# Spectral mixing and a leaky-ReLU MLP: zero-tile matmuls and a reordered prologue

## The chip, the cores and the metric

The kernel runs on one core of one Trainium2 chip. The metric is the device time of one execution in microseconds (us), lower is better. Engines are named as in the profile: PE is TensorE, ACT is ScalarE, DVE is VectorE, POOL is GpSimd and SP is SyncE. Each runs its own list of instructions in the order in which the program wrote them; waits between them are semaphores.

## The reference

The input x has 8 batches of 3008 positions with 256 features. Every feature column is transformed along the positions, multiplied by a complex filter, and transformed back. The result is 24,064 tokens of 256 features for a two-layer MLP.

```python
X = np.fft.rfft(x, axis=1)
F = (filt_r + 1j * filt_i)[None, :, :]
y = np.fft.irfft(X * F, n=x.shape[1], axis=1)
h = y.reshape(B * S, D) @ w_in            # 256 -> 2048
out = np.maximum(0.01 * h, h) @ w_out     # 2048 -> 256
```

Inputs and output are float32; inside, the kernel works in float16 with float32 accumulation.

## The kernel before, in words

**Two kinds of work.** The transform is split as 3008 = 94 x 32 and done by matmuls against constant matrices. The MLP works on 47 chunks of 512 tokens. While the MLP of one batch runs, the transform of the next is threaded into it by a table of slots (`plan`, lines 399 to 412, run by the loop at line 424). Only the first batch has nothing to hide behind: its transform is written out by hand, lines 314 to 345, and is called the prologue here. The change touches only the prologue and the loads ahead of it.

**The stages of the prologue.** The 256 features are cut in two halves of 128 (`hf` 0 and 1), so that one half can be loaded while the other is worked on.

- **S1** (`first_s1`, line 247, matmuls at line 251): 94-point transforms. Eight groups per half, four 128-column matmuls each, from x_sb and the constant f1_sb into a PSUM bank. ACT or DVE then copies the bank into big[0] (`spread`, line 181). Groups 0 to 3 need the first half of x's columns, groups 4 to 7 the second.
- **T1** (`t1_part`, line 193): DVE transposes of 32x32 blocks, two per half, after all eight copies.
- **S2** (`first_s2`, line 256, matmuls at line 260): 32-point transforms of 4 or 8 columns of frequencies, then both products with the filters. On the POOL path ACT copies the bank to an SBUF tile fx of the pool's tags p1 and p2 (line 268, two buffers each) and POOL multiplies (line 271). On the DVE path DVE multiplies from PSUM (line 276). S2(hf, c) is written for the call that begins with column c: c = 8 and 20 of half 0 and c = 8 of half 1 go to POOL, the others to DVE. All S2 results share the two wide banks, named ph. The products are called fy.
- **upper** (line 306): copies a filter half from partitions 0 to 63 to 64 to 127, fa on ACT and fb on DVE (line 308), once that half is loaded. The products need it.
- **SA** (`first_sa`, line 279, matmuls at line 284): the inverse 32-point transform of fy, two accumulating matmuls of 512 columns for four columns of frequencies, copied by ACT into big[2] (line 285).
- **T2** (`first_t2`, line 292): four transposes on DVE, parts 0 and 1 after all SA of half 0, parts 2 and 3 after half 1.
- **SB** (`first_sb`, line 294, matmuls at line 301): inverse 94-point transforms in 16 groups, copied into yt (line 304), groups 0 to 7 by ACT and 8 to 15 by ACT and DVE in turn. With the last copy the MLP's first matmuls (line 365) can run.
- **keep_warm** (line 311): matmuls whose result nobody reads, into po_ps; before, they read small_sb and i1_sb.

**The loads.** SP issues the four parts of f1_sb and small_sb. POOL issues all others, in this order: two x loads of half 0, two each of fa and fb of half 0 (`filt_load`, line 137), the same six for half 1, then i1_sb and w_in_sb. POOL's transfers have eight completion semaphores in turn, so the ninth transfer is issued after the first has landed, and so on. In the kernel before the ninth is the first fa load of half 1.

The order around the change in the kernel before is: S1, T1, upper and S2 of half 0; the eight S1 groups of half 1; x_load(1); T1 of half 1; upper(1); SA(0,0) and SA(0,16); S2(1,8) and S2(1,0); SA(0,8) and SA(0,20); S2(1,16); SA of half 1 with T2; SB.

Of the kernel before, what the change touches and what calls it, by code (L numbers as in the profile page):

```python
# [10 lines left out]
P = 128  # L11
FP16 = mybir.dt.float16
# [6 lines left out]
N1, N2 = 94, 32  # L19
NC = 24  # L20
Q = 32
R1 = 96
# [43 lines left out]
def kernel(  # L66
# [9 lines left out]
    nc = tc.nc  # L76
    B, N, D = x.shape
# [5 lines left out]
    CH = 512  # L83
# [11 lines left out]
    i1_sb = cpool.tile([P, N2, N1], FP16, name="i1_sb")  # L95
    small_sb = cpool.tile([P, 3, P], FP16, name="small_sb")
# [5 lines left out]
    big = [cpool.tile([P, Q * D], FP16, name=f"big{i}") for i in range(3)]  # L102
# [3 lines left out]
    scrp = ctx.enter_context(tc.tile_pool(name="scr", bufs=2))  # L106
# [7 lines left out]
    po_ps = psp.tile([P, 2, D], FP32, name="po_ps")  # L114
    turn = {"ph": 0, "pf": 0}

    def bank(kind, n, w):
        of = wide if kind == "ph" else single
        t = of[turn[kind] % len(of)]
        turn[kind] += 1  # L120
        return t[:, : n * w].rearrange("p (n w) -> p n w", n=n)
# [4 lines left out]

    DH = D // 2

    def x_load(b, n0=0, nn=N2, d0=0, dn=D):

        for lo, cnt in ((0, R1),) if b + 1 < B else ((0, 64), (64, N1 - 64)):
            nc.gpsimd.dma_start(  # L132
                x_sb[lo : lo + cnt, ds(n0, nn), ds(d0, dn)],
                bass.AP(tensor=x.tensor, offset=x.offset + (b * N + lo * N2 + n0) * D + d0,
                        ap=[[N2 * D, cnt], [D, nn], [1, dn]]))

    def filt_load(dst, src, d0, dn):

        for q, first, sgn in ((0, 0, 1), (Q, N1, -1)):
            nc.gpsimd.dma_start(  # L140
                dst[q : q + Q, :, ds(d0, dn)],
                bass.AP(tensor=src.tensor, offset=src.offset + first * D + d0,
                        ap=[[N1 * D, N2 // 2], [sgn * NC * D, 2], [sgn * D, NC], [1, dn]]))
# [5 lines left out]
    nc.sync.dma_start(small_sb[:], small_d.ap())  # L149
    for hf in range(2):  # L150
        for n0 in (0, N2 // 2):
            x_load(0, n0, N2 // 2, hf * DH, DH)
        filt_load(fa_sb, filt_r, hf * DH, DH)
        filt_load(fb_sb, filt_i, hf * DH, DH)
    nc.gpsimd.dma_start(i1_sb[:], i1_d.ap())
# [2 lines left out]
    one = cpool.tile([1, 1], FP32, name="one")  # L158
    nc.vector.memset(one[:], 0.0)
    nc.scalar.activation(one[:], one[:], AF.Lrelu)  # L160

    nc.vector.memset(big[2][:].rearrange("p (e n t) -> p e n t", n=Q, t=2)[:, :, NC:Q, :], 0.0)


    def s1_group(b, g, copy=nc.scalar.copy):
# [10 lines left out]
    def paired(t):  # L176
        return t[:].rearrange("p (e n t) -> p n e t", n=Q, t=2)

    def spread(dst, n0, ps, copy, e0=0):
        nn, de = ps.shape[1], ps.shape[2] // 2  # L180
        copy(paired(dst)[:, ds(n0, nn), ds(e0, de)], ps.rearrange("p n (e t) -> p n e t", t=2))  # L181
# [3 lines left out]
    def t1_part(b, i, flat=False):  # L185
        def go():
            a = big[(4 * b) % 3][:].bitcast(FP32)[:, ts(i, E4 * Q)].rearrange("p (e n) -> p e n", n=Q)
            o = big[(4 * b + 1) % 3][:].bitcast(FP32)
            if flat:
                o = o[:, ts(i, E4 * Q)].rearrange("p (e n) -> p e n", n=Q)  # L190
            else:
                o = o.rearrange("p (n e) -> p e n", n=Q)[:, ts(i, E4), :]
            nc.vector.transpose(o, a)  # L193
        return go
# [52 lines left out]
    def first_s1(hf, g, kind, copy):  # L247
        ps = bank(kind, 4, DH)
        for j in range(4):
            n2 = 4 * g + j  # L250
            nc.tensor.matmul(ps[:, j, :], f1_sb[:N1, n2, :], x_sb[:N1, n2, ts(hf, DH)],  # L251
                             start=True, stop=True)
        spread(big[0], 4 * g, ps, copy, hf * DH // 2)


    def first_s2(hf, c, n, on_pool):
        ps = bank("ph", n, DH)
        src = paired(big[1])
        for j in range(0, n, 4):
            nc.tensor.matmul(ps[:, ds(j, 4), :].rearrange("p n (e t) -> p n e t", t=2), fwd2,  # L260
                             src[:, ds(c + j, 4), ts(hf, DH // 2)], start=True, stop=True)
        fs = [f[:, ds(c, n), ts(hf, DH)] for f in (fa_sb, fb_sb)]
        if on_pool:
            y = [outp.tile([P, n, DH], FP16, tag="ost", name=f"fy{i}_h{hf}_c{c}") for i in range(2)]
            xs = [scrp.tile([P, 4, DH], FP32, tag=f"p{j // 4 + 1}", name=f"fx_h{hf}_c{c + j}")
                  for j in range(0, n, 4)]
            for j, xf in enumerate(xs):
                act(xf[:], ps[:, ts(j, 4), :])
            for i in range(2):
                for j, xf in enumerate(xs):  # L270
                    nc.gpsimd.tensor_tensor(y[i][:, ts(j, 4), :], xf[:], fs[i][:, ts(j, 4), :], AL.mult)
        else:
            y = [ypp.tile([P, n, DH], FP16, tag=f"yw{i}", bufs=2, name=f"fy{i}_h{hf}_c{c}")
                 for i in range(2)]
            for i in range(2):
                nc.vector.tensor_tensor(y[i][:], ps, fs[i], AL.mult)  # L276
        ys[(hf, c)] = y

    def first_sa(hf, c):
        y = ys.pop((hf, c))  # L280
        for j in range(0, y[0].shape[1], 4):
            ps = bank("pf", 4, DH)
            for i, m in enumerate((inv2, inv2x)):
                nc.tensor.matmul(ps, m, y[i][:, ds(j, 4), :], start=(i == 0), stop=(i == 1))  # L284
            act(paired(big[2])[:, ds(c + j, 4), ts(hf, DH // 2)],
                ps.rearrange("p n (t e) -> p n e t", t=2))
# [7 lines left out]
    def first_sb(g, copy, kind):  # L294
        dt, h = g // 8, g % 8
        src = big[0][:].rearrange("p (h n e r t) -> p h n r t e", h=2, n=Q // 2, r=2, t=2)
        ps = bank(kind, 4, N1)
        for j in range(4):
            n2 = 4 * h + j
            for t in range(2):  # L300
                nc.tensor.matmul(ps[64 * t : 64 * t + 64, j, :], src[:, dt, n2 // 2, n2 % 2, t, :],  # L301
                                 i1_sb[:, n2, :], start=True, stop=True)
        yv = yts[0][:, dt, :].rearrange("p (a c) -> p a c", c=N2)
        copy(yv[:, :, ds(4 * h, 4)], ps.rearrange("p c a -> p a c"))  # L304

    def upper(hf):
        for t, cp in ((fa_sb, act), (fb_sb, dve)):
            cp(t[64:P, :, ts(hf, DH)], t[0:64, :, ts(hf, DH)])


    def keep_warm(n):
        for _ in range(n):
            nc.tensor.matmul(po_ps.rearrange("p a d -> p (a d)"), small_sb[:, 0, :],  # L313
                             i1_sb[:].rearrange("p a d -> p (a d)")[:, 0:512],
                             start=True, stop=True)

    for g in range(8):
        first_s1(0, g, two[(g // 2) % 2], (act, dve)[g % 2])
    t1_part(0, 0, True)(), t1_part(0, 1, True)()
# [1 line left out]
    first_s2(0, 8, 8, True)  # L321
    first_s2(0, 0, 8, False)
    first_s2(0, 20, 4, True)
    first_s2(0, 16, 4, False)
    for g in range(8):
        first_s1(1, g, two[g % 4 == 3], dve if g in (3, 5, 7) else act)
    x_load(1)
    t1_part(0, 2, True)(), t1_part(0, 3, True)()
    upper(1)
    first_sa(0, 0), first_sa(0, 16)  # L330
    first_s2(1, 8, 8, True)
    first_s2(1, 0, 8, False)
    nc.gpsimd.dma_start(w_out_sb[:], moe_w_out.rearrange("(ct p) d -> p ct d", p=P))
    first_sa(0, 8), first_sa(0, 20)
    first_s2(1, 16, 8, False)
    first_sa(1, 0)
    first_t2(0), first_t2(1)
    first_sa(1, 16), first_sa(1, 8)
    first_t2(2), first_t2(3)
    keep_warm(5)  # L340
    for g in range(8):
        first_sb(g, act, two[(g // 2) % 2])
    keep_warm(3)
    for g in range(8, 16):
        first_sb(g, (act, dve)[g % 2], two[(g // 2) % 2])

# [52 lines left out]
    def plan(b, s1, per, t1, s2, step, lag, t2, sb):  # L399
        for g in range(16):  # L400
            at(s1 + g // per, s1_group(b, g, dve if b == 1 and g % 2 else act))
        if b + 1 < B:
            at(s1 + 15 // per, lambda: x_load(b + 1))
        for i in range(4):
            at(t1 + i, t1_part(b, i))
        for g in range(12):
            at(s2 + (step * g) // 4, s2_group(b, g))
            at(s2 + lag + (step * g) // 4, sa_group(b, g))
        for i in range(4):
            at(t2 + i, t2_part(b, i))  # L410
        for g in range(16):
            at(sb + g // 2, sb_group(b, g, dve))
# [6 lines left out]
    for slot in range(SL * (NCHUNK + 1)):  # L419
        ci, g = divmod(slot, SL)  # L420
# [36 lines left out]
```

## Time and profile before

| what | value |
|---|---|
| median of 3 runs | 785.25 us (784.58 to 785.80) |
| profiled execution, own time | 787.67 us |
| its span | 785.9 us |
| PE busy | 763.0 us, 97% of the span |
| ACT, DVE, POOL busy | 557.0, 365.1, 150.7 us |
| first S1 matmul | 9.59 us |
| first S2 matmul | 17.67 us |
| first SB matmul | 39.80 us |
| end of the last yt copy of the prologue | 45.98 us |

Times in the trace are counted from the start of the span. A row of the timeline gives the start, the duration, the engine and line, and what was written from what. "x8" at its end means that eight like instructions were merged, and the brackets give the idle time of that engine just before and what ended it. The names of tiles are shown without their numbers, so big, pf, ph and yt stand for several buffers.

### The profile page before, as it was taken

The page shows a single profiled execution, that of the slowest core. Times are in us where ns is not written, and L with a number is a line of the kernel's source. Part 1 is how long each engine was busy: PE and PEld are TensorE (multiplying, and loading weights), DVE is VectorE, ACT ScalarE, POOL GpSimd, SP SyncE. Part 2 cuts the span into 40 slices and gives each one's busy share as a digit, 9 for nine tenths or more (in the row PEclk, how much of TensorE's full clock was granted, in tenths as well). Part 3 has the DMA queues.
Part 4 walks back from the last instruction along what each step waited for, and adds up shares of the span by engine and source line. Part 5 has one row for each costly group of instructions (what it writes and reads, how often), then busy time and mean ns, then how long its engine had stood idle before and what let it go on. Part 6 is the DMA issues. An engine that isn't in the chain of part 4 may idle for free.

```text
span 785.9 us, 13623 instructions
## 1 busy us (share of the span) xinstructions
PE 763.0 (97%) x5812; PEld 528.6 (67%) x5812; DVE 365.1 (46%) x459; ACT 557.0 (71%) x794; POOL 150.7 (19%) x122
## 2 busy tenths in 40 slices
PE   2799999999999999999999999999999999999998
PEld 1356677666776677866777667776677667676666
DVE  3869760784327652387316754078432765200000
ACT  3686768676687767877687775967668776666664
POOL 5773400240003400052001410024000340000000
PEclk9999999999999999999999999999999999999999
DMA  9943010501032010501014101050100101101111
GB/s 174 214 59 94 28 42 28 122 28 41 28 79 70 28 41 28 119 31 41 28 41 108 41 28 41 28 120 28 42 28 28 41 28 42 41 28 41 41 41 54
DMA packets 42013, 43.39 MB, mean 55 GB/s; under 512 B 14274, under 2 KB 40514, under 8 KB 41282
## 3 DMA queue, kind: packets, MB, share of 16 engines
q0 software_dynamic: 15760, 16.99, 13.2%
q1 hardware_dynamic: 26192, 25.53, 9.3%
q8 instruction: 45, 0.74, 0.4%
q14 instruction: 16, 0.13, 0.1%
HBM read 34.10 MB, written 24.64 MB: 75 GB/s over the span
## 4 chain that ended last, share of the span: by engine, by line
PE 93%; ACT 2%; issue 1%; DVE 0%; ACTq 0%; DVEq 0%
PE po_ps L379 41%; PE ph L365 40%; PE pf L170 3%; PE pf L237 2%; PE pf L210 2%; PE pf L225 2%; PE pf L379 1%; ACT big L181 1%; ACT gt_c L370 1%; PE pf L284 1%; PE ph L260 0%; PE ph L301 0%; DVE fy_h_c L276 0%; PE po_ps L313 0%; PE pf L301 0%
## 5 line engine op out<-in xcount | busy, mean ns | idle before, releaser
L370 ACT ACTIVATE gt_c<-ph 128x1024 f16<-128x1024 f32 x376 | 384.8, 1024 | 194.8 <-PE ph L365 193.8
L365 PE MATMUL ph<-yt,w_in_sb 128*128 128x512 f16 (+7 forms) x1728 | 386.6, 351 | 0.4 <-ACT yt L304 0.2
L379 PE MATMUL po_ps<-w_out_sb,gt_c 128*128 128x256 f16 x2944 | 381.5, 272 | 0.6 <-ACT ost_c_t L386 0.6
L379 PEld LDWEIGHTS <-gt_c 128*128 128x128 f16 x3008 | 290.7, 98 | 86.7 <-issue 1.7
L365 PEld LDWEIGHTS <-w_in_sb 128*128 128x128 f16 x1728 | 163.0, 98 | 95.2 <-issue 1.0
L218 POOL TENSOR_TENSOR y_b_g<-p_b_g,p_b_g 128x512 f16<-128x512 f32 x84 | 106.9, 1273 | 225.5 <-DVE p_b_g L216 225.5
L181 ACT CAST big<-pf 128x512 f16<-128x512 f32 x195 | 111.8, 606 | 11.8 <-PE pf L251 11.7
L193 DVE STREAM_TRANSPOSE big<-big 128x1024 f32<-128x1024 f32 x32 | 55.8, 1846 | 127.1 <-ACT big L181 126.7
L240 DVE CAST yt<-pf 128x376 f16<-128x376 f32 x112 | 56.3, 545 | 85.9 <-PE pf L237 85.9
L214 DVE TENSOR_TENSOR p_b_g<-pf,fa_sb 128x512 f32<-128x512 f32 x84 | 58.1, 692 | 38.0 <-PE pf L210 35.5
L386 ACT COPY ost_c_t<-po_ps 128x256 f32<-128x256 f32 x184 | 69.4, 377 | 6.7 <-PE po_ps L379 5.6
L201 DVE STREAM_TRANSPOSE big<-big 128x1024 f32<-128x1024 f32 x28 | 51.1, 1936 | 34.5 <-ACT big L181 34.5
L215 DVE TENSOR_TENSOR p_b_g<-pf,fb_sb 64x512 f32<-64x512 f32 x84 | 58.2, 693 | 1.1
L216 DVE TENSOR_TENSOR p_b_g<-pf,fb_sb 64x512 f32<-64x512 f32 x84 | 57.4, 683 | 1.1
L132 POOL DMA_DIRECT2D x_sb<-in_x_dram x12 | 8.5, 713 | 256.6 <-PE pf L170 255.5
L237 PEld LDWEIGHTS <-big 128*128 128x128 f16 x448 | 25.7, 98 | 13.2
L170 PE MATMUL pf<-x_sb,f_sb 94*128 94x256 f16 x224 | 33.8, 272 | 0.1
L210 PE MATMUL pf<-big,small_sb 128*128 128x512 f16 x84 | 31.8, 379 | 0.0
L225 PE MATMUL pf<-y_b_g,small_sb 128*128 128x512 f16 x84 | 31.8, 379 | 0.0
L237 PE MATMUL pf<-i_sb,big 128*128 128x94 f16 x448 | 28.7, 206 | 0.0
L170 PEld LDWEIGHTS <-f_sb 94*128 94x128 f16 x224 | 21.0, 97 | 9.5 <-issue 1.3
L347 POOL TENSOR_SCALAR fb_sb<-fb_sb 64x6144 f16<-64x6144 f16 x1 | 15.7, 15742 | 0.4 <-DVE fy_h_c L276 0.4
(45 smaller groups left out, 142.8 us busy)
## 6 DMA issues: line engine op xcount, KB each, us to landing
out_dram<-ost_c_t SPq DMA_DIRECT2D x92, 256.0 KB, 2.1
x_sb<-in_x_dram POOLq DMA_DIRECT2D x6, 1536.0 KB, 11.3
x_sb<-in_x_dram POOLq DMA_DIRECT2D x4, 384.0 KB, 11.0
w_in_sb<-in_moe_w_in_dram POOLq DMA_DIRECT2D x1, 1024.0 KB, 14.9
w_out_sb<-in_moe_w_out_dram POOLq DMA_DIRECT2D x1, 1024.0 KB, 10.2
x_sb<-in_x_dram POOLq DMA_DIRECT2D x1, 1024.0 KB, 9.1
f_sb<-fwd_const SPq DMA_DIRECT2D x4, 192.0 KB, 3.2
fa_sb<-in_filt_r_dram POOLq DMA_DIRECT2D x4, 192.0 KB, 9.8
```

The source lines that it names most:

```text
L170: nc.tensor.matmul(ps[:, j, :], f1_sb[:N1, n2, :], x_sb[:N1, n2, :], start=True, stop=True)
L181: copy(paired(dst)[:, ds(n0, nn), ds(e0, de)], ps.rearrange("p n (e t) -> p n e t", t=2))
L214: nc.vector.tensor_tensor(p1[:], ps, fa, AL.mult)
L215: nc.vector.tensor_tensor(p2[0:64], ps[64:P], fb[64:P], AL.mult)
L216: nc.vector.tensor_tensor(p2[64:P], ps[0:64], fb[0:64], AL.mult)
L218: nc.gpsimd.tensor_tensor(y1[:], p1[:], p2[:], AL.add)
L237: nc.tensor.matmul(ps[:, j, :], src[:, dt, n2, :], i1_sb[:, n2, :], start=True, stop=True)
L240: copy(yv[:, :, ds(4 * h, 4)], ps.rearrange("p c a -> p a c"))
L365: nc.tensor.matmul(ph[:, j, ds(o, ln)], w_in_sb[:, dt, ts(ct, P)], yts[b % 2][:, dt, ds(lo, ln)], start=(dt == 0), stop=(dt == NDT - 1),)
L370: nc.scalar.activation(gts[ci][:, ds(2 * g, 2), :], ph, AF.Lrelu)
L379: nc.tensor.matmul(po, gts[ci][:, ct, ts(tj, P)], w_out_sb[:, ct, :], start=(ct == 0), stop=(ct == NCT - 1))
L386: nc.scalar.copy(ost[:, tj % 2, :], po)
```

## The change

- 24 matmuls of a zeroed 128x512 tile are issued on PE ahead of everything else. The tile, `idle`, is a buffer of tag p1; one memset on DVE fills it, and the memset of big[2] follows after it. `keep_warm` now reads this tile, also in its later use.
- The two x loads of half 0 are each cut into two, of 64 and of 32 partitions. So there are four x loads ahead of the filters, and the ninth transfer on POOL is the first x load of half 1.
- upper(1) moves from after T1 of half 1 to before S1 of half 1.
- S2(0,16) moves from before S1 of half 1 to between its groups 2 and 3.
- S2(1,16) moves ahead of SA(0,8) and SA(0,20).
- keep_warm(3) between SB groups 7 and 8 is removed.

```diff
-    def x_load(b, n0=0, nn=N2, d0=0, dn=D):
+    def x_load(b, n0=0, nn=N2, d0=0, dn=D, parts=None):
 
-        for lo, cnt in ((0, R1),) if b + 1 < B else ((0, 64), (64, N1 - 64)):
+        if b + 1 < B:
+            parts = parts or ((0, R1),)
+        for lo, cnt in parts or ((0, 64), (64, N1 - 64)):
...
         for n0 in (0, N2 // 2):
-            x_load(0, n0, N2 // 2, hf * DH, DH)
+            x_load(0, n0, N2 // 2, hf * DH, DH, None if hf else ((0, 64), (64, 32)))
...
-    nc.vector.memset(big[2][:].rearrange("p (e n t) -> p e n t", n=Q, t=2)[:, :, NC:Q, :], 0.0)
...
     def keep_warm(n):
         for _ in range(n):
-            nc.tensor.matmul(po_ps.rearrange("p a d -> p (a d)"), small_sb[:, 0, :],
-                             i1_sb[:].rearrange("p a d -> p (a d)")[:, 0:512],
+            nc.tensor.matmul(po_ps[:].rearrange("p a d -> p (a d)"), idle[:, 0:P], idle[:],
                              start=True, stop=True)
 
+    idle = scrp.tile([P, CH], FP16, tag="p1", name="idle")
+    nc.vector.memset(idle[:], 0.0)
+    keep_warm(24)
+
+    nc.vector.memset(big[2][:].rearrange("p (e n t) -> p e n t", n=Q, t=2)[:, :, NC:Q, :], 0.0)
...
     first_s2(0, 20, 4, True)
-    first_s2(0, 16, 4, False)
+    upper(1)
     for g in range(8):
+        if g == 3:
+            first_s2(0, 16, 4, False)
         first_s1(1, g, two[g % 4 == 3], dve if g in (3, 5, 7) else act)
     x_load(1)
     t1_part(0, 2, True)(), t1_part(0, 3, True)()
-    upper(1)
     first_sa(0, 0), first_sa(0, 16)
     first_s2(1, 8, 8, True)
     first_s2(1, 0, 8, False)
     nc.gpsimd.dma_start(w_out_sb[:], moe_w_out.rearrange("(ct p) d -> p ct d", p=P))
+    first_s2(1, 16, 8, False)
     first_sa(0, 8), first_sa(0, 20)
-    first_s2(1, 16, 8, False)
...
         first_sb(g, act, two[(g // 2) % 2])
-    keep_warm(3)
```

## The prediction

> **What bounds the kernel now.** I read the page first, then the order of events in the first 60 us. The page says that TensorE (PE) is busy 97% of the span, and its strip of 40 slices has only two slices short of full, the first 39 us. From the chain of waits, PE carries everything from 56.7 us to the end without a gap, so nothing touched by this change can alter that stretch; the change can only move the moment at which it begins. The prediction is therefore about the prologue, which ends with the last copy into yt at 45.98.
>
> From the page:
>
> ```profile
> PE   2799999999999999999999999999999999999998
> ```
>
> The timeline of VectorE (DVE), prologue rows (start, duration, what, idle before):
>
> ```profile
> 17.55 0.95 DVE L308 COPY fb_sb<-fb_sb 64x3072 f16<-64x3072 f16 x1
> 20.78 1.22 DVE L276 TENSOR_TENSOR fy_h_c<-ph,fb_sb 128x1024 f16<-128x1024 f32 x1
> 22.68 0.69 DVE L276 TENSOR_TENSOR fy_h_c<-ph,fa_sb 128x512 f16<-128x512 f32 x1 [0.68 <-PE ph L260]
> 26.88 2.37 DVE L193 STREAM_TRANSPOSE big<-big 128x1024 f32<-128x1024 f32 x2
> 29.29 0.96 DVE L308 COPY fb_sb<-fb_sb 64x3072 f16<-64x3072 f16 x1
> 31.29 1.23 DVE L276 TENSOR_TENSOR fy_h_c<-ph,fa_sb 128x1024 f16<-128x1024 f32 x1 [1.04 <-ACT fx_h_c L268]
> 34.70 1.22 DVE L276 TENSOR_TENSOR fy_h_c<-ph,fa_sb 128x1024 f16<-128x1024 f32 x1 [1.06 <-PE ph L260]
> ```
>
> PE, the same stretch:
>
> ```profile
> 12.45 1.01 PE L251 MATMUL pf<-x_sb,f_sb 94*128 94x128 f16 x8 [0.99 <-DMA x_sb<-in_x_dram]
> 22.05 0.59 PE L260 MATMUL ph<-big,small_sb 128*128 128x512 f16 x1 [1.61 <-DVE fy_h_c L276]
> 29.31 1.88 PE L260 MATMUL ph<-big,small_sb 128*128 128x512 f16 x4 [1.33 <-DVE big L193]
> 31.02 2.74 PE L284 MATMUL pf<-fy_h_c,small_sb 128*128 128x512 f16 x6
> 34.41 1.04 PE L284 MATMUL pf<-fy_h_c,small_sb 128*128 128x512 f16 x4
> ```
>
> The reader should see three things. The second-half S1 groups wait at 22.05 behind one S2 matmul that DVE releases. The last S2 (L260, 33.55) waits behind six SA matmuls, so DVE starts its last products only at 34.70. And PE runs at half speed: four 128x512 matmuls take 1.88 us (0.43 each) until about 34.2, then four take 1.04 (0.22 each beyond the last one's tail).
>
> The arrivals of the filters, not marked in those rows, decide my forecast. The DMA answer for the window around 14.1 us is
>
> ```profile
> fb_sb<-in_filt_i_dram POOLq DMA_DIRECT2D x2, 192.0 KB, 10.6
> ```
>
> The two are the second-half fb loads, issued at 13.39 and 14.10; with 10.3 and 10.8 us to landing they are there at 23.7 and **24.9**. The second-half fa loads (9.84 + 11.7 and 12.69 + 9.9) land at 21.5 and 22.6, the second-half x loads at 18.3 and 21.1. In the kernel before these are wanted at 26.3 (ACT) and 29.3 (DVE), so they hide.
>
> **The skill.** "TensorE: Matmul & The Clock Gate", Part 1 (the HAM clock gate): a matmul takes N/1.2 ns while cold and N/2.4 + 2.5 ns warm, warmth needs a busy window of about 3.4 us, and an idle window returns it to cold. The trace agrees on the prices (0.43 and 0.22 us at N = 512); how long warmth outlasts sparse work no row of before shows. The same page, under the array's architectural detail, says that ACT and DVE are strict FIFO; the rows agree, each engine's order being the program's. "DMA: Bandwidth & Descriptors", Anatomy of one DMA: the semaphore follows the last byte by most of a fixed 2 us. Here the queue carries a steady 717 packets per us from 8 to 22 us; the 256-byte packets (12,288) are through at about 22.7 and the last filter load lands at 24.9, 2.2 later.
>
> **The change, part by part.**
>
> *24 zero matmuls.* They start after one small memset, about 1.4 us. All cold: 24 x 0.427 = 10.2, ending at 11.6; warm after 3.4 to 6.8 us: 7 to 8.5. First x lands at 9.6. If warm, S1's second quarter finishes sooner (16 matmuls at about 0.06 instead of 0.107), so DVE's last copy starts about 13.8 instead of 14.36, the transpose at 14.5 instead of 15.15, four S2 matmuls take 0.87 instead of 1.71, and DVE's fy pair ends near 20.4 instead of 22.0. Gain here 1.6, all spent by the next part. If cold: gain 0, same end.
>
> *upper(1) moved ahead of the second-half S1.* The built order puts DVE's fb copy between fy(0,0) and fy(0,16), and ACT's fa copy ahead of all its second-half S1 copies. DVE stands from 20.4 until the fb load lands, 24.9. Queued behind it on DVE: fy(0,16), three S1 copies, the transpose. So 24.95 + 0.93 copy, + 2 x 0.60 products, + 3 x 0.60 S1 copies, last one's tail: transpose at **29.0** instead of 26.88. ACT waits to 22.6, copies until 25.4, and its five S1 copies (0.53 each, two held by buffers) end by 28.3, under DVE's 28.9. Loss: 2.1. The copy no longer stands at 29.29, but DVE was idle there.
>
> *S1 groups 0 to 2 ahead of S2(0,16).* They run at 19 to 20 instead of 22.46; worth nothing, since ACT copies them only after 25.4.
>
> *idle holds one of the two p1 buffers* until its last use. The order shows fx(0,20) now waiting on POOL: three products of 1.11 from about 18.2, so 21.6. ACT's next item waits to 22.6 anyway: 0.
>
> *S2(1,16) ahead of SA(0,8), SA(0,20).* Transpose ends 29.0 + 2.37 = 31.4. Four S2 matmuls, cold: 1.71 + 0.18, fy(1,0) at 33.35 (31.29 before). S2(1,16) follows when ACT has emptied its buffer, 33.6 to 34.5, so DVE goes straight on: fy(1,16) at 33.35 + 2.28 = **35.65**, against 34.70. The six SA matmuls (2.56) no longer stand in DVE's way. Recovered: 1.15 of the 2.1.
>
> *End of the prologue.* fy(1,16) ends 38.0; SA(1,16) and SA(1,8), eight warm matmuls, 38.1 to 39.8 (38.8 before); keep_warm(5) 1.08; SB at 41.0 (39.80 before). ACT's eight yt copies (0.37 each) pace what follows, so dropping keep_warm(3) gives back only 0.1 to 0.4 of its 0.75. Sum: +1.2 - 0.2 = +1.0.
>
> *First x load split.* Issue of 1,536 descriptors takes 1.08, of 768 0.71, so 64 rows about 0.83: the first piece leaves 0.25 earlier. But PE needs both pieces, and the queue is saturated later. The x second-half loads are now issued after the first piece lands (about 9) instead of at 6.3; packets ahead of them last to 14, so nothing starves. Bounds -1.3 (packets at the full rate from 4 us on) to +1 (a queue that starves once); I take 0, because the filters' last packet is set by the sum of the packets.
>
> *x_load(1), w_out, the fb negation on POOL:* each about 2 later at most; x lands about 41 for use at 47.7, w_out at 48 for 59, the negation ends 54 for use at 66. Hidden; the next wait they could cause is PE's S1 of batch 1, 5 us away.
>
> The profiled execution has 787.67 for a span of 785.9; it becomes about 788.7. The runs' median is 785.25, so **786.3**. About 0.2% (1.6 us) is what a measurement can tell here.
>
> **Rivals.**
> 1. *PE stays cold longer, clearly slower.* PE has almost nothing from 22.8 to 26 (S1 group 4 needs ACT's first copy), so warmth is lost; in before it took from 29.31 to 34.2 to come back, and the denser start is now 31.4 or 33.6. If it returns at 38 the loss is 1.6, at 40 2.4, at 42 3.4: SA(1,16), SA(1,8) and the five warmers then run at 0.43. It decides above 0.2% from 38 us on. For it: 33.6 plus 4.9 is 38.5. Against: SA runs from 28.3 already.
> 2. *Warm throughout: no change.* Zero matmuls and the earlier S1 keep the clock: S2(1,x) takes 0.87, fy(1,0) at 32.5; total +0.2, with the edge of an earlier issue 0.0 to 0.2: 785.3. Against: the idle stretches of 3.5 us near 13.5 to 17 and of 3 near 23.
> 3. *Transfers earlier: faster.* Two pieces in flight fill the queue from 4 us; all landings 1.3 earlier, the DVE wait ends at 23.6, and with it total 0.0 (cold) to -1.1 (warm): 784.2.
> 4. *The zero matmuls don't release the clock.* Then the first half is as before, fy ends 22.0, still before 24.9: the same +1.0, because DVE waits anyway.
>
> **How the numbers follow.** Forecast, with rival 4 in it (+0.3 to +1.5; own range 785.5 to 786.8): 0.50. Rival 1 (+1.6 to +3.4): 0.27. Rival 2: 0.13. Rival 3: 0.05. A loss that I don't see, over 1.6: 0.05. Slower by over 0.2%: 0.27 + 0.05 + 0.03 of the forecast's upper edge = 0.35. Faster: most of rival 3 and a little for a gain I don't see, 0.06. Within: 0.59. The range, 784.7 to 788.3, holds the forecast, rival 2 and rival 1 up to a loss of 3.0.
>
> **What would show it.** DVE's second fb copy starting at 24.5 to 25, with some 4 us of idle ahead put down to the fb load; the second transpose pair near 29.0; the last fy pair following the one before without a gap, at 35.7; SB's first matmul near 41. Wrong if the fb load lands before 23, if 128x512 matmuls take 0.22 from 31 us (rival 2) or still 0.43 after 38 (rival 1), or if PE's steady stretch after 57 us is itself longer.

## The result, and the profile after

The changed kernel takes **787.94 us** (median of 6 runs, 787.46 to 788.42). The kernel before, run beside it, takes 785.52 (6 runs, 784.58 to 787.19). The ratio is 1.0028, with a 95% interval of 1.0015 to 1.0041: slower by 2.2 us, between 1.2 and 3.2. The forecast was 786.3 in a range of 784.7 to 788.3. So the direction and the range held, and the likeliest case, +1.0, was too small by more than half. The prediction gave 0.59 to a change of at most 0.2% and 0.35 to a loss above that; 0.28% lies above it, though the interval reaches below.

The steady stretch is not the cause. From the end of the last yt copy to the end of the span there are 739.9 us in the kernel before (785.9 - 45.98) and 739.8 after (785.7 - 45.85). So the difference is to be looked for in the prologue. These two executions alone don't show it, since both prologues end near 45.9; the second profile of before, below, does.

The timeline of DVE after, the prologue rows that answer to those shown of before:

```profile
15.15 0.95 DVE L308 COPY fb_sb<-fb_sb 64x3072 f16<-64x3072 f16 x1
18.38 1.21 DVE L276 TENSOR_TENSOR fy_h_c<-ph,fb_sb 128x1024 f16<-128x1024 f32 x1
23.76 0.95 DVE L308 COPY fb_sb<-fb_sb 64x3072 f16<-64x3072 f16 x1 [4.16 <-DMA fb_sb<-in_filt_i_dram]
24.74 0.69 DVE L276 TENSOR_TENSOR fy_h_c<-ph,fa_sb 128x512 f16<-128x512 f32 x1
27.93 2.37 DVE L193 STREAM_TRANSPOSE big<-big 128x1024 f32<-128x1024 f32 x2
32.27 1.22 DVE L276 TENSOR_TENSOR fy_h_c<-ph,fa_sb 128x1024 f16<-128x1024 f32 x1 [1.97 <-PE ph L260]
34.54 1.21 DVE L276 TENSOR_TENSOR fy_h_c<-ph,fa_sb 128x1024 f16<-128x1024 f32 x1
```

DVE is done with the first products at 19.6 and then stands for 4.16 us until the second-half fb filter has landed. Everything behind the copy waits with it: the products of S2(0,16), three S1 copies, the transposes at 27.93. The last pair of products (34.54) follows the pair before without a gap.

ACT over the same stretch, after:

```profile
20.41 0.59 ACT L268 COPY fx_h_c<-ph 128x512 f32<-128x512 f32 x1 [3.02 <-POOL fy_h_c L271]
21.46 2.75 ACT L308 COPY fa_sb<-fa_sb 64x3072 f16<-64x3072 f16 x1 [0.47 <-DMA fa_sb<-in_filt_r_dram]
24.23 2.07 ACT L181 CAST big<-pf 128x512 f16<-128x512 f32 x4
```

ACT loses time in three places ahead of its first second-half S1 copy: 3.02 us for a buffer that POOL holds, 0.47 us for the fa load, and 2.75 us for the fa copy itself.

PE, after:

```profile
1.23 7.43 PE L313 MATMUL po_ps<-idle 128*128 128x512 f16 x24 [1.23 <-DVE idle L317]
10.63 0.61 PE L251 MATMUL pf<-x_sb,f_sb 94*128 94x128 f16 x8 [1.08 <-DMA x_sb<-in_x_dram]
15.26 1.88 PE L260 MATMUL ph<-big,small_sb 128*128 128x512 f16 x4 [3.58 <-DVE big L193]
24.89 1.57 PE L251 MATMUL pf<-x_sb,f_sb 94*128 94x128 f16 x12 [3.46 <-ACT big L181]
33.45 5.56 PE L284 MATMUL pf<-fy_h_c,small_sb 128*128 128x512 f16 x18
```

The zero matmuls do speed up S1 (0.61 us for eight instead of 1.01). S2 still takes 1.88 for four, as before. At 24.89 S1 group 4 of half 1 has stood for 3.46 us, until ACT could free a PSUM bank for it.

The chain of work that ended last says it in two rows (start, duration, what):

```profile
5.09 7.59 DMA fa_sb<-in_filt_r_dram
...
12.96 10.70 DMA fb_sb<-in_filt_i_dram
```

Two filter loads carry the chain from 5.1 to 23.7 us, with 0.28 us between them: a first-half fa load, whose landing lets POOL issue the second-half fb load, and then that load. The kernel before never waited for the second of them. It did not have it earlier either: in the second profile of before it was issued at 13.10 and took 10.6 us, so it landed at 23.7 too. What changed is not the load but the moment at which its copy is asked for.

### The profile page after: what moved, and what is told of

It is laid out like the page before. It is cut to its first block, busy times and chain, and to the rows that moved or that the text cites. A ratio compares the mean times of both kernels' runs of the same rounds, so it can differ in the third digit from the quotient of the medians.

```text
span 785.7 us, 13669 instructions
## 1 busy us (share of the span) xinstructions
PE 769.0 (98%) x5833; PEld 529.6 (67%) x5833; DVE 364.7 (46%) x460; ACT 556.9 (71%) x794; POOL 151.9 (19%) x124
## 4 chain that ended last, share of the span: by engine, by line
PE 93%; DMA 2%; ACT 2%; issue 1%; DVE 1%; POOL 0%; ACTq 0%; DVEq 0%; POOLq 0%
PE po_ps L383 41%; PE ph L369 40%; PE pf L170 3%; PE pf L237 2%; PE pf L225 2%; PE pf L210 2%; DMA fb_sb<-in_filt_i_dram 1%; DMA fa_sb<-in_filt_r_dram 1%; PE pf L383 1%; ACT big L181 1%; PE pf L284 1%; ACT gt_c L374 1%; POOL x_sb L134 0%; PE ph L260 0%; ACT yt L304 0%
```

## The experiments

Each ratio below is against the kernel before on the same chip, with its 95% interval; 0.1% is 0.79 us.

### The kernel before, once more

No edit. The profile of before that the prediction reads took 787.67, which is above all six runs of before in the result; this asks what another execution looks like.

> The kernel before once more, for a second profile. Theory F (filter wait: the change loses because upper(1) makes DVE wait for the second-half fb load) says nothing on it. Theory C (clock phase: the profile of before that the prediction read was one of the slow executions, and most executions of before get a warm PE earlier) expects a span of 783 to 784.5 instead of 785.9, the 128x512 matmuls of S2 in half 1 at 0.22 us instead of 0.43 or warming before 32 us, and the last yt copy ending at 43.5 to 45 instead of 45.98. If the profile is again at 45.9 to 46.1 and still cold to 34, C falls.

Measured: 785.76 against 786.07, ratio 1.0000 (0.9991 to 1.0010). The 35 runs of the kernel before on that chip lie between 784.06 and 788.12. This profile's own time is 784.98, its span 783.2. DVE of this execution of the kernel before:

```profile
25.33 2.37 DVE L193 STREAM_TRANSPOSE big<-big 128x1024 f32<-128x1024 f32 x2
...
30.86 1.21 DVE L276 TENSOR_TENSOR fy_h_c<-ph,fb_sb 128x1024 f16<-128x1024 f32 x1
32.00 1.22 DVE L276 TENSOR_TENSOR fy_h_c<-ph,fa_sb 128x1024 f16<-128x1024 f32 x1
```

and PE of the same execution:

```profile
29.45 1.48 PE L284 MATMUL pf<-fy_h_c,small_sb 128*128 128x512 f16 x6
30.77 1.02 PE L260 MATMUL ph<-big,small_sb 128*128 128x512 f16 x2
```

Same program, another prologue. The second transposes start at 25.33, not 26.88, because the first two x loads had landed at 8.55 and 10.89 instead of 9.59 and 12.45. And the six SA matmuls ahead of S2(1,16) take 1.48 us, not 2.74, so the gap of 1.06 us on DVE ahead of the last products (34.70 in the first profile) does not exist here: 32.00 follows directly. The windows of the two executions of before give the reason for the second difference. The columns are the stretch, its length, the busy times of PE, PE's weight loads, DVE, ACT and POOL, the granted clock (the share of TensorE's full clock that the profile records), the DMA share and GB/s. First the profile that the prediction used:

```profile
29.00:33.00 4.00, 3.69 (x9) 1.16 (x9) 2.93 (x4) 3.26 (x8) 1.79 (x2) 0.70 1.09 229
33.00:36.00 3.00, 2.48 (x9) 0.74 (x8) 1.94 (x3) 2.08 (x4) 3.00 (x4) 0.83 1.14 246
```

then this one:

```profile
29.00:33.00 4.00, 3.82 (x14) 1.23 (x12) 3.28 (x3) 3.15 (x7) 3.35 (x3) 1.00 1.12 237
```

The granted clock was 0.70 in one and 1.00 in the other. The last yt copy ends at 43.27 instead of 45.98. The kernel before has prologues that differ by 2.7 us, and the prediction was built on the long one. The second one is no norm either: its own time lies 0.8 below the median of its runs.

### The change with upper(1) back in its old place

Later texts call this kernel e2.

```diff
-    upper(1)
     for g in range(8):
...
     t1_part(0, 2, True)(), t1_part(0, 3, True)()
+    upper(1)
```

> The changed kernel with upper(1) back after T1 of half 1, all else as changed. Theory F: DVE's 4.2 us wait before the second fb copy goes, the second transpose pair starts at 23 to 25 instead of 27.93, the last yt copy ends 2 to 3.5 us earlier than in the changed kernel (42.5 to 44), time 784 to 785.7: 2.2 to 3.9 under the changed kernel's 787.9. Theory C (only clock phases differ): within 0.8 of the changed kernel.

Measured: 783.91 against 786.07, ratio 0.9982 (0.9974 to 0.9990), faster than before. DVE:

```profile
24.61 2.37 DVE L193 STREAM_TRANSPOSE big<-big 128x1024 f32<-128x1024 f32 x2
```

Everything else of the change together is worth -0.18%; with upper(1) early it is +0.28%. So the early upper costs 0.46%, 3.6 us, by these two ratios. In the profiles, the transposes move from 24.61 to 27.93 (3.3) and the last yt copy ends at 42.20 against 45.85 (3.6).

### upper(1) early, and nothing else

The kernel before, with upper(1) ahead of S2(0,16).

```diff
     first_s2(0, 20, 4, True)
+    upper(1)
     first_s2(0, 16, 4, False)
...
     t1_part(0, 2, True)(), t1_part(0, 3, True)()
-    upper(1)
```

> The kernel before with only upper(1) moved ahead of S1 of half 1. Theory F: DVE waits for fb (lands 24 to 25), the second transpose pair at 28.5 to 29.2 instead of 26.9, the six SA matmuls still ahead of S2(1,16); 1.0 to 2.5 slower than before: 786.5 to 788. Theory C: within 0.8 of before.

Measured: 789.56 against 786.07, ratio 1.0053 (1.0040 to 1.0067), +4.2 us by the ratio: more than expected. DVE:

```profile
25.03 1.41 DVE L308 COPY fb_sb<-fb_sb 64x3072 f16<-64x3072 f16 x1 [3.52 <-DMA fb_sb<-in_filt_i_dram]
...
29.66 2.37 DVE L193 STREAM_TRANSPOSE big<-big 128x1024 f32<-128x1024 f32 x2
```

The early copies, with nothing else of the change, give more than the whole loss. The load landed at 25.0 here and at 23.7 in the changed kernel, so the transposes are 4.3 later than in the second profile of before (25.33) and the last products, at 36.28 against 32.00, also 4.3.

### Which of the two copies does it

Two kernels, each the changed one with one of the two copies put back. `of` picks 0 for ACT's fa copy, 1 for DVE's fb copy.

```diff
-    def upper(hf):
-        for t, cp in ((fa_sb, act), (fb_sb, dve)):
+    def upper(hf, of=(0, 1)):
+        for t, cp in [((fa_sb, act), (fb_sb, dve))[i] for i in of]:
...
-    upper(1)
+    upper(1, (0,))          # fa early; the other kernel has (1,)
...
     t1_part(0, 2, True)(), t1_part(0, 3, True)()
+    upper(1, (1,))          # fb late; the other kernel has (0,)
```

Only ACT's fa copy early (e7):

> The changed kernel with only DVE's fb copy of upper(1) back after T1 of half 1; ACT's fa copy stays ahead of its S1 copies. Theory F-DVE (DVE's wait for fb carries the loss): DVE no longer stands, but ACT waits for fa to 21.5 and copies to 24.2, so S1's copies end near 27 and T1 starts at 26.5 to 27.2 instead of 27.9; 0.7 to 1.5 under the changed kernel: 786.4 to 787.2. Rival F-ACT (ACT's part carries it): within 0.4 of the changed kernel. Rival: ACT's part costs nothing: 784, as with upper(1) undone.

Measured: 787.49 against 785.68, ratio 1.0022 (1.0014 to 1.0030). DVE of that kernel:

```profile
26.23 0.69 DVE L181 CAST big<-pf 128x512 f16<-128x512 f32 x1 [3.85 <-PE pf L251]
...
27.88 2.37 DVE L193 STREAM_TRANSPOSE big<-big 128x1024 f32<-128x1024 f32 x2
```

and PE:

```profile
25.05 1.56 PE L251 MATMUL pf<-x_sb,f_sb 94*128 94x128 f16 x12 [3.47 <-ACT big L181]
```

Only DVE's fb copy early:

> The changed kernel with only ACT's fa copy of upper(1) back after T1 of half 1; DVE's fb copy stays early. With e7 this is the second half of the pair. Theory either (each early copy alone holds S1 as long as both): DVE waits for fb to 23.7, then fy(0,16), three S1 copies, T1 at 27.8 to 28.1; ACT's fa copy now stands between its S1 copies and the SA copies; 787.3 to 788.5. Theory F-ACT (only ACT's copy carries the loss): 784 to 785.

Measured: 788.47 against 785.33, ratio 1.0036 (1.0022 to 1.0050). DVE and then PE of that kernel:

```profile
24.05 0.95 DVE L308 COPY fb_sb<-fb_sb 64x3072 f16<-64x3072 f16 x1 [4.23 <-DMA fb_sb<-in_filt_i_dram]
...
28.23 2.37 DVE L193 STREAM_TRANSPOSE big<-big 128x1024 f32<-128x1024 f32 x2
```

```profile
26.38 0.58 PE L251 MATMUL ph<-x_sb,f_sb 94*128 94x128 f16 x4 [3.04 <-DVE fy_h_c L276]
```

Either copy alone gives the loss of both, within the intervals, with the transposes at 27.88 and 28.23 against 27.93. With fa early ACT frees its first S1 bank late, PE waits for the bank, and DVE waits 3.85 us for PE. With fb early DVE waits for the load and PE for DVE. The two waits stand side by side, so taking one away gains nothing that clears the intervals. A reader who sees only the 4.16 us on DVE, and moves only that copy back, gets nothing for it.

### The other parts, one at a time

The zero tile, its 24 matmuls and keep_warm reading it, on the kernel before (keep_warm's operands and the place of big[2]'s memset as in the change, not shown again):

```diff
+    idle = scrp.tile([P, CH], FP16, tag="p1", name="idle")
+    nc.vector.memset(idle[:], 0.0)
+    keep_warm(24)
```

> The kernel before with only the zero tile, its 24 matmuls and keep_warm reading it. The 24 take 7 to 10 us and end before the first S1; S1 at 0.06 us a matmul instead of 0.107; the first S2 at 17.0 instead of 17.67. Theory F: 0 to 0.7 faster than before, since the first half has little slack without the early upper. Theory C: the clock is the whole difference, so this alone changes the time by over 1 us either way. If the idle buffer matters (fx(0,20) waits for POOL), ACT's third fx copy starts near 22 instead of 20.5 and S1 group 3 of half 1 shifts with it, cost up to 1.

Measured: 785.18 against 786.07, ratio 0.9992 (0.9982 to 1.0001). The 24 matmuls take 8.01 us; S1 follows them without a gap at 9.08, though the first x load had landed by 8.55, when POOL issued the load that waits for it. So here they hold the first four S1 groups up by some 0.5 us, which costs nothing, since the next four wait for x until 10.58. Eight S1 matmuls take 0.61. The second transposes start at 24.43, 0.9 earlier than in the second profile of before, but the six SA matmuls take 2.43 in this execution and DVE's last products start at 31.95, after 0.77 us of waiting for S2: 0.05 earlier than in that profile. The gain at the transposes was given back behind the SA matmuls.

The split x load, on the kernel before (with x_load's `parts` as in the change):

```diff
-            x_load(0, n0, N2 // 2, hf * DH, DH)
+            x_load(0, n0, N2 // 2, hf * DH, DH, None if hf else ((0, 64), (64, 32)))
```

> The kernel before with only the two x loads of half 0 cut into 64 and 32 partitions. Theory N (the cut is neutral: the packets' sum sets every arrival, and the arrivals differ from run to run anyway): within 0.7 of before, the second-half fb load landing at 23.5 to 25. Theory S (the cut brings the first x earlier, as the profile after the change seems to show, 8.49 against 9.59): 1 to 1.5 faster. A loss of over 0.7 would speak for the semaphores: the x loads of half 1 issued later, at 7.8 instead of 6.3, would then be late for S1.

Measured: 785.07 against 785.68, ratio 0.9997 (0.9989 to 1.0005): nothing. x is there at 8.68 and 10.97, against 8.55 and 10.89 in the second profile of before.

S2(1,16) ahead of SA(0,8) and SA(0,20), on the kernel before:

```diff
+    first_s2(1, 16, 8, False)
     first_sa(0, 8), first_sa(0, 20)
-    first_s2(1, 16, 8, False)
```

> The kernel before with only S2(1,16) ahead of SA(0,8) and SA(0,20). The prediction's sum gave it 1.15 with a PE that is cold to 34 us. Theory C: in most executions of before the clock is back by 30 us (as in the second profile of before), so that DVE's last two pairs already follow one another, and the gain is 0 to 0.5. If it is 1.0 or more, the prediction's size stands.

Measured: 785.00 against 785.68, ratio 0.9994 (0.9986 to 1.0003): 0.5 us faster, and the interval includes no change. In its profile the last products start at 31.69 without a gap; in the second profile of before there is none either.

The three, -0.08, -0.03 and -0.06%, add up to -0.17%. The kernel with upper(1) put back, which also lacks keep_warm(3) and has the other S1 order, has -0.18%. No run tests these two parts alone.

### The zero tile in a buffer of its own

With upper(1) late, as above, and the zero tile no longer one of the two p1 buffers (this kernel is called e8):

```diff
-    idle = scrp.tile([P, CH], FP16, tag="p1", name="idle")
+    idle = cpool.tile([P, CH], FP16, name="idle")
```

> upper(1) back after T1 of half 1 as in e2, and the zero tile in a buffer of its own instead of one of tag p1. If the p1 buffer costs what e2's profile shows (ACT idle 3.0 us before the third fx copy, its S1 copies from 21.1 on), those copies start by 18.7 to 19.5, the second transpose pair at 23.5 to 24.0 instead of 24.6, and the time is 0.5 to 1.0 under e2: 782.9 to 783.4. If the buffer costs nothing, as the prediction had it, within 0.3 of e2.

Measured: 783.23 against 785.68, ratio 0.9973 (0.9964 to 0.9982). ACT of that kernel:

```profile
18.15 0.59 ACT L268 COPY fx_h_c<-ph 128x512 f32<-128x512 f32 x1 [0.68 <-PE ph L260]
18.63 1.60 ACT L181 CAST big<-pf 128x512 f16<-128x512 f32 x3
```

The third fx copy waits 0.68 us for PE and no longer 3 us for POOL, and the second-half S1 copies start at 18.63 instead of 21.12. The transposes move from 24.61 to 23.54, SB from 36.37 to 35.68. The borrowed buffer costs 0.7 us (0.0009 of the ratio; the two intervals overlap, so the profiles carry this more than the times). In the changed kernel itself that wait is covered, since ACT stands until the fa load has landed anyway.

### PE kept busy through the gaps

The kernel with its own zero tile, with fillers (e10), that is, zero matmuls put into PE's idle stretches: keep_warm(4) ahead of S1 group 4, 13 after S1 of the first half, 4 ahead of S2(0,16), 8 after SA(0,16). It asks whether S2's 0.43 us each is the cold clock, as the prediction took it.

```diff
     for g in range(8):
+        if g == 4:
+            keep_warm(4)
         first_s1(0, g, two[(g // 2) % 2], (act, dve)[g % 2])
+    keep_warm(13)
...
+            keep_warm(4)
             first_s2(0, 16, 4, False)
...
     first_sa(0, 0), first_sa(0, 16)
+    keep_warm(8)
```

> e8 with 29 more zero matmuls put where PE stood idle: 4 between the two x pieces of S1, 13 after S1 of half 0, 4 ahead of S2(0,16), 8 after SA(0,16). Theory W (the clock fell back because PE stood still from 9.5 to 10.7 and from 11.9 to 15.3): the four S2 matmuls at 15.3 take 1.04 instead of 1.88, those at 26 too, T1 of half 1 at 22.7 instead of 23.5, the last yt copy ends at 39 to 40 instead of 41.5; 781 to 782. Rival: the clock doesn't stay, the fillers run at 0.43 and hold S2 up, 13 x 0.43 = 5.6 us after 11.9, so S2 at 17.5; 785 or more. Between: the clock stays but the fillers hold up the matmuls behind them, 783.

Measured: 783.46 against 785.33, ratio 0.9978 (0.9969 to 0.9986), as without the fillers. PE:

```profile
11.93 2.97 PE L313 MATMUL po_ps<-idle 128*128 128x512 f16 x13
15.67 1.88 PE L260 MATMUL ph<-big,small_sb 128*128 128x512 f16 x4 [0.77 <-DVE big L193]
18.27 0.85 PE L251 MATMUL pf<-x_sb,f_sb 94*128 94x128 f16 x12
```

The fillers next to S2 run at 0.22 us each and the S1 matmuls after it at full pace, but four S2 matmuls take 1.88, to the hundredth what they take in every profile above. The changed kernel itself shows the same; its four-matmul S2 stretches are

```profile
15.20:17.20 2.00, 1.88 (x4) 0.51 (x5) 0.90 (x1) 1.19 (x3) 1.22 (x2) 0.50 1.83 181
30.30:32.30 2.00, 1.88 (x4) 0.44 (x4) 0.03 (x1) 0.81 (x2) 0.14 (x1) 1.00 1.20 256
```

with the granted clock at 0.50 in the first and at 1.00 in the second. The S1 matmuls right behind the first take 1.42 us for twelve, against 0.85 with fillers, so the clock was indeed at half there. The clock is not what makes S2 slow, and half the clock doesn't make it slower.

### S2 with another reading pattern

The same kernel, and S2's moving operand (the one streamed through the array; the weights are the other) read as 512 neighbouring elements of big[1] instead of 256 pairs that stand 128 bytes apart. S2 then multiplies the wrong elements of the first batch, so only the time is to be read.

```diff
-            nc.tensor.matmul(ps[:, ds(j, 4), :].rearrange("p n (e t) -> p n e t", t=2), fwd2,
-                             src[:, ds(c + j, 4), ts(hf, DH // 2)], start=True, stop=True)
+            nc.tensor.matmul(ps[:, ds(j, 4), :].rearrange("p n e -> p (n e)"), fwd2,
+                             big[1][:, ds(hf * Q * DH + (c + j) * DH, 4 * DH)], start=True, stop=True)
```

> e10 with S2 of the first batch reading 512 consecutive elements of each partition of big[1] instead of 256 pairs of elements 128 bytes apart; so its products are of the wrong elements and the first batch's output is not the reference's, all instructions and waits being the same. Theory P (the pattern of the operand halves the pace of these matmuls, whatever the clock): the four S2 matmuls take 1.04 instead of 1.88 both times, the two of S2(1,16) 0.6, everything behind comes 1.5 to 1.9 earlier: 781.5 to 782. Theory K (they are slow because the clock is cold just then): still 1.88, 783.4.

Measured: 781.31 against 785.75, ratio 0.9945 (0.9932 to 0.9959). PE:

```profile
14.56 1.03 PE L260 MATMUL ph<-big,small_sb 128*128 128x512 f16 x4
...
24.46 1.03 PE L260 MATMUL ph<-big,small_sb 128*128 128x512 f16 x4
```

Four now take 1.03 instead of 1.88, 0.22 instead of 0.43 for each further one. It is the pattern. Whether the distance between the pairs or their number is what costs, this run doesn't separate.

### The version that beats both

The kernel with its own zero tile and upper(1) late, without the five warming matmuls ahead of SB:

```diff
     first_t2(2), first_t2(3)
-    keep_warm(5)
```

> e8 without keep_warm(5) ahead of SB. SB starts when T2's second part ends, 34.9, instead of 35.7; groups 8 to 15 wait for T2's last part at 37.9 as in e8, so most of it isn't kept: 0 to 0.5 under e8's 783.2. If the clock falls for want of the five, SB is slower and the time above 783.5.

Measured: 782.79 against 785.75, ratio 0.9964 (0.9950 to 0.9978). SB's first matmul starts at 34.99 instead of 35.68:

```profile
34.99 0.70 PE L301 MATMUL pf<-i_sb,big 128*64 128x94 f16 x16 [0.60 <-DVE big L292]
```

It is the fastest kernel here whose output is the reference's, 0.36% under the kernel before. That it is better than the one with keep_warm(5), 0.9973, is not shown: the two intervals overlap.

## Why the prediction was right or wrong

The sums below take the second profile of before (784.98) against the profile after (787.50): the difference of these two executions, 2.52, is near that of the medians, 2.42.

| step | forecast | second profile of before to after | measured |
|---|---|---|---|
| second transposes | +2.1 | 25.33 to 27.93 | +2.60 |
| from there to the last products | -1.15 | 6.67 to 6.61 | -0.06 |
| from there to SB | +0.25 | 5.08 to 5.48 | +0.40 |
| SB to the end of the last yt copy | -0.2 | 6.19 to 5.83 | -0.36 |
| sum | +1.0 | 43.27 to 45.85 | +2.58 |

**The mechanism was right.** "DVE stands from 20.4 until the fb load lands, 24.9": it stood from 19.6 to 23.76, 4.16 us, and what was queued behind it is the list that the prediction gives. The kernel with only upper(1) restored, 3.6 us below the changed one, shows that this move and no other part makes it slower, and the kernel before with this move alone, 1.0053, shows it from the other side. The forecast that ACT's copies end just under DVE's (28.3 and 28.9) was also right in kind: either copy alone is enough.

**The term that failed is "Recovered: 1.15 of the 2.1".** S2(1,16) ahead of the SA matmuls was to take 1.06 us of waiting off DVE. That wait is in the profile that the prediction read, where the six SA matmuls took 2.74 at a granted clock of 0.70. In the second profile of before they take 1.48 at 1.00 and there is no wait to recover. Alone, the move gave 0.5 us (interval from -0.2 to 1.1). The wait is not in every execution: of the five profiled executions with the old order of S2(1,16) it stands in two, 1.06 us in the first profile of before and 0.77 with the zero tile alone. The prediction took a row of one execution for a property of the kernel, and it had a warning: that execution's own time, 787.67, stood 2.4 above the median of the runs.

**The transposes' +2.1 was too small by 0.5,** for the same reason: it started from 26.88, where the second profile of before has 25.33. That the load landed at 23.7 instead of 24.9 took 1.2 of this back. The absolute times in the list of what would show the step are all about 1 us too late for it: 24.5 to 25 was 23.76, 29.0 was 27.93, 35.7 was 34.54, 41 was 40.02.

**"Gain here 1.6" in the first half was too large.** It held for S1 (0.06 us each, as forecast), but 0.84 of it was to come from four S2 matmuls in 0.87 instead of 1.71. They take 1.88 in the kernel with fillers, where PE is warm on both sides, so that part was never there. It did no harm to the sum, since the filter wait swallowed the first half's gain, as the prediction said. What the first half did gain shows where DVE's first products end: 19.59 in the changed kernel against 20.45 in the second profile of before, so 0.9, of which 0.26 is x's second piece being there sooner (10.63 against 10.89).

**Rival 1** (PE cold for longer) is a small part of the result. Two stretches of the changed kernel, with the clock in the third column from the end:

```profile
13.00:19.00 6.00, 3.44 (x16) 1.75 (x17) 4.83 (x5) 3.58 (x3) 4.25 (x5) 0.50 1.82 181
...
33.00:36.00 3.00, 3.00 (x9) 1.02 (x8) 3.00 (x4) 1.23 (x2) 3.00 (x4) 0.50 1.18 251
```

The clock is at half in both; between them it came up twice (from 19.1 to 22.5 and from 29.3 to 32.8), and from 36.2 on it is full: before the 38 us from which this rival was to decide. (The prediction took the S2 matmuls from 29.31 on as the start of a cold stretch of 4.9 us in the kernel before; the record of that profile is at half only from 30.6 to 34.0, and S2's pace tells nothing of the clock.) The stretch from the last products to SB is 0.40 longer, and DVE's last transposes wait 0.66 us for ACT's SA copies where the second profile of before has 0.36. The kernels with and without fillers bear out that the clock is the reason: e8, at half clock from 28.5 to 31.9, has 5.48 for this stretch and 0.72 for the wait; e10, at full clock throughout, has 5.08 and 0.34. **Rival 2** fell by the same rows. **Rival 3** (earlier landings) fell in its sign: fb did land at 23.7, near its 23.6, but the second profile of before shows x landing as early without the split, and the split alone did nothing. **Rival 4** fell too: the zero matmuls do bring the clock up, 24 of them in 7.43 us.

The range held in part by luck. It had been widened for rival 1, up to a loss of 3.0, and by the table rival 1's cause is about 0.4 us of the result; the likeliest case's own range, 785.5 to 786.8, was missed.

The steps costed at nothing held as far as they were tested: the split load (0.9997), and the p1 buffer as long as upper(1) is early. The S1 groups ahead of S2(0,16) were tested by no run alone. With upper(1) late the buffer's cover is gone and it costs 0.7. Dropping keep_warm(3) was to give 0.1 to 0.4; the stretch from SB to the last yt copy is 0.36 shorter.

What stays open is why two executions of one program have x 1.0 to 1.6 us apart in landing. The six runs of the changed kernel lie within 1.0 us, the six of the kernel before beside them within 2.6; that the wait for the filters absorbs what differs in front of it would fit, but no run tests it.

## What to carry to other kernels

Before an instruction is moved forward on an engine that works in order, put the landing of its data (here 23.7 to 25.0) beside the time at which the engine is ready for it (19.6); the difference is paid by everything queued behind, and where two engines get such a wait at once, only removing both helps. Before a gap is counted as recoverable, compare the profiled execution's own time with the median: if it stands 2 us above, as here, some of its gaps may belong to that execution and not to the kernel. And a matmul at half pace is not yet a cold clock: look whether another matmul beside it runs at full pace, and whether its own pace changes where the clock does.

## What the hardware showed that was not expected

- **A moving operand in small pieces halved TensorE's pace, and then the clock did not matter.** Pairs of 2-byte elements, 128 bytes apart, cost 0.43 us for 128x512, at a recorded clock of 1.00 and of 0.50 alike; 512 neighbours cost 0.22 at 1.00. The Trainium skill, "SBUF — State Buffer", section "Door 1: The DMA port swizzle (why `[64,N]` ≈ `[32,N]`)", has a note that consecutive accesses to one 16-byte line run at full bandwidth, that this needs at least two to a line, and that each crossing to a new line pays. The run agrees in direction: two elements to a line cost twice the time of eight. Two to a line, if each element counts as one access, were not enough here. That lines are the reason no run shows. The pattern was worth 0.33% (0.9945 against 0.9978).
- **Half pace has two causes that look alike.** The cold price, 0.43, is the same number as the price of the scattered operand, which is why the prediction mixed them up. "TensorE: Matmul & The Clock Gate", Part 1, names an idle window of about 3.4 us as what sends the clock back. In the changed kernel the recorded clock falls to 0.50 at 12.3, 0.6 us after the last S1 matmul of the half (11.7). With upper(1) back in place it falls at 11.2, while S1 is still running; in the 3.4 us before that PE was busy for 1.87. So in these runs the clock fell after sparse work, without an idle window of that length.
- **The record of the clock can say full speed where the pace is half.** The second profile of before has it at 1.00 throughout its prologue. Yet eight S1 matmuls take 1.01 us there at 8.55, where they take 0.61 after the zero matmuls, and six SA matmuls take 2.77 at 24.29, where six take 1.48 at 29.45. The durations are the better witness there.
